# Splitting the second token half of a pair of d_ff tiles in one 768-wide piece, with sum and rectifier in one VectorE operation

## The chip, the core and the metric

The kernel runs on one core of a Trainium2 chip. The metric is device microseconds of one execution, lower is better. The times are medians of several executions; the profile is of one execution of its own. In the profile PE is TensorE's matmul, PEld its weight load, DVE is VectorE, ACT is ScalarE, POOL is GpSimd and SP is SyncE, whose queue issues the DMAs.

## What is computed

```python
def _moe_ref(x, w_in, w_out, s, b):      # 2304 tokens, d_model 512, d_ff 2048
    h = x @ w_in
    r = np.maximum(h, 0.0)
    g = s * (r * r) + b
    return g @ w_out
def _moe2_ref(x, w_in, w_out, alpha):
    h = x @ w_in
    g = np.maximum(h, 0.0) + alpha * np.minimum(h, 0.0)
    return g @ w_out
def reference(...):
    x = attention over a window of 64 (batch 4, 8 heads, 576 positions, head size 64)
    return _moe2_ref(_moe_ref(x, ...), ...)
```

So: a windowed attention, then layer one (code: layer 0; rectifier, then a square), then layer two (code: layer 1; a leaky rectifier with a slope for each d_ff unit). Activations stand transposed, with d_ff or d_model on the 128 partitions and tokens along the free axis.

## The kernel before

**Split operands.** Each fp32 operand of a matmul is split in a rounded high part and a low part (value minus high part), and a product is three matmuls: high by high, high by low, low by high. For a tile of the hidden activation g the split is a copy that rounds (`gh`, line 1048) and a subtraction (`gl`, line 1051), both in `halves`.

**Stages.** From 0 to about 240 us the attention and two d_ff groups of layer one run block by block (lines 1336 and 1396 hold their matmuls). From there on the work goes in *pairs*: two d_ff tiles of 128 by two token halves of 384 tokens are one pair, and `hidden_pair` computes its four 128 x 384 results of `x @ w_in` with seven half-size products instead of eight (`product`, matmuls on line 978, six matmuls each). Three token passes q of 768 tokens run over each d_ff group. Layer one has five such pairs in each pass (groups of 4, 2 and 4 tiles), 15 in all; layer two has four in groups 0 and 1, 12 in all, and another 12 in groups 2 and 3, which take a path of their own (`seven`) with seven products in the second matmul too.

**Inside a pair.** The products accumulate in four PSUM banks: two of a ring of two buffers (`b1`, `b4`, in the profile the tile `h`), and the two halves of a tile of its own (`hb`, in the profile `ab`). ACT copies between them (line 989): `b1` to `hb` half 0, `b4` to SBUF (`p5`), `hb` half 0 to half 1, `hb` half 1 to `b4`. At the end the first token half of the pair lies in `b1` (first d_ff tile) and `b4` (second tile), and the second token half is `hb` plus `p5`: a 768-wide DVE addition (line 1006) writes it to `both`, a stretch of 768 columns of the SBUF area `aq`, 384 for each d_ff tile. A PSUM buffer of the ring is given to the next pair once its last reader has run.

**After it, layer one.** `square` calls `squared` for each of the four 384-wide results: rectifier (line 1058, ACT or DVE) into a tile `r`, square in place (line 1062, ACT or DVE), then `halves`. In layer two `lrelu` calls `leaky` (a scaled copy on ACT, line 1075, and a DVE operation, line 1078, into `r`) and then `halves`. `g_place` gives the 768 columns for high and low part in the area `ax`.

**Second matmul.** `project` (line 1419) multiplies a tile's `gh` and `gl` with w_out, 12 matmuls for each tile of 128 x 384, about 1.7 pairs behind the pair that made it, and `sums` adds the PSUM result to the output (lines 1492 to 1499).

**Weights.** w_in and w_out arrive as float64; `converted` loads one tile (line 664, 512 KB, three buffers), ACT reads both words (lines 668 and 672, both wait for the load), DVE makes the exponent (lines 677 and 678), joins the words (682) and adds them (687). A buffer is free for the load after next but one when line 687 has run. w_out of layer one is then scaled (738 on ACT, 741 on DVE) and added up on POOL (733).

**Order.** Nothing waits for a free engine at run time. `Plan.step` takes the ways in which a step can run (engine and assumed cost), what it reads and writes, and a due time `at`; `emit` goes through all steps once and fixes both the engine and the order on each engine. A change of one step's cost or number thus moves others. On the chip every engine runs its list strictly in order.

Of the kernel before, what the change touches and what calls it, by code (L numbers as in the profile page):

```python
# [8 lines left out]

F32 = mybir.dt.float32  # L10
F32R = mybir.dt.float32r
# [3 lines left out]
AF = mybir.ActivationFunctionType  # L15
# [3 lines left out]
P = 128  # L19
# [5 lines left out]
HALF = 384  # L25
# [6 lines left out]
HURRY = 12.0  # L32
# [6 lines left out]
GRING = 10  # L39
# [19 lines left out]
def f32(ap):  # L59
    return ap.bitcast(F32)  # L60
# [188 lines left out]
def tile_window_attention_two_mlps(  # L249
# [14 lines left out]
    nc = tc.nc  # L264
# [27 lines left out]
    T = Plan()  # L292
# [4 lines left out]
    XA = area("ax", 8 * NT)  # L297
# [7 lines left out]
    XW = 4 * HALF  # L305
# [15 lines left out]
    def act(cols, fn):  # L321
        return ("act", 0.2 + cols * 0.00084, fn, 0.0)

    def dve(cols, fn, fast=False, port=False):
        return ("dve", 0.15 + cols * (0.00053 if fast else 0.00106), fn, 0.0) + (True,) * (fast or port)
# [15 lines left out]
    for g in range(SPLIT[0]):  # L341
        for bi in range(NB):
            n = blocks[bi][1]
# [13 lines left out]
    with tc.manual_schedule():  # L357
# [49 lines left out]
        for x, kind in enumerate(ROW):  # L407
            if x != 2 and kind == "mm":
                T.step([("pool", 0.35, lambda x=x: nc.gpsimd.tensor_copy(caps[:, x, :], caps[:, 2, :]), 0.0)],
                       reads=["caps2"], writes=[f"caps{x}"], at=-15.0, after=CONST_AT)  # L410
# [407 lines left out]
        C = 2 * HALF  # L818
        x2 = lambda ap: ap.rearrange("p (k c) -> p k c", k=2)
# [127 lines left out]
        def hidden_pair(layer, g, q, p):  # L947
            fs = groups[layer][g]
            n = number[layer, g, p]
            pr = f"{layer}.{g}.{q}.{p}"  # L950
            t0 = begin[layer, g, q] + p * unit(layer, g)
            slot = unit(layer, g) / 7
            seven = (layer, g) in SEVEN
# [12 lines left out]
            p5 = T.place("p5." + pr, AQ, 4 * HALF + n % 2 * HALF, HALF)  # L966
# [20 lines left out]
            def copy(out, src, reads, writes, order):  # L987
# [14 lines left out]
            copy(b4_, b3_, [hb3], [b4], 4)  # L1002
            product(4, 6, b4_, b4, False)
            both = T.place("c." + pr, AQ, C, C)
            T.step(
                [dve(C, lambda: nc.vector.tensor_add(  # L1006
                    x2(T[both]), T["hb"][:, :, :HALF],
                    T[p5].rearrange("p (o c) -> p o c", o=1).to_broadcast([P, 2, HALF])))],
                reads=[hb2, hb3, p5], writes=[(both, 0), (both, 1)], at=t0 + 5 * slot - HURRY,
            )  # L1010
            c_ = lambda x: (lambda: T[both][:, x * HALF:(x + 1) * HALF])
            f1, f2 = fs[2 * p], fs[2 * p + 1]
# [8 lines left out]
            for c, i, f, hk, hn, order in outs:  # L1021
                at = t0 + order * slot
                if seven:
                    leaky(f"B{(c if f == f1 else 3 - c)}.{g}.{q}.{p}", f, hk, hn, at)
                elif layer == 1:
                    g_place(layer, g, q, c, i, f)
                    lrelu(g, q, c, i, f, hk, hn, at)
                else:
                    g_place(layer, g, q, c, i, f)
                    square(q, c, f, hk, hn, at)  # L1030

        ORDER = (1, 5, 6, 2, 7, 3, 4)

        def g_place(layer, g, q, c, i, f):
            key = f"{layer}.{2 * q + c}.{f}"
            if i == 0 and c == 0:
                g_place.n += 2 * len(groups[layer][g])
            n = g_place.n + c * len(groups[layer][g]) + i
            G = T.place("g" + key, XA, 7 * XW + n % GRING * 2 * HALF, 2 * HALF, F32R)
            gh, gl = "gh" + key, "gl" + key  # L1040
            T.parts[gh] = T.parts[gl] = G
            T.tiles[gh], T.tiles[gl] = (lambda: T[G][:, :HALF]), (lambda: T[G][:, HALF:])

        g_place.n = 0

        def halves(key, r, rn, n, at):
            gh, gl = "gh" + key, "gl" + key
# [20 lines left out]
        def square(q, c, f, hk, hn, at):  # L1068
            squared(f"0.{2 * q + c}.{f}", hk, hn, HALF, at)

        def leaky(r, f, hk, hn, at):
            leaky.n += 1
            r2 = T.place(f"r2.{leaky.n}", AQ, leaky.n % 2 * HALF, HALF)
            rn, r2n = (lambda: T[r][:, :HALF]), (lambda: T[r2])
            T.step([act(HALF, lambda: nc.scalar.activation(r2n(), hn(), AF.Identity, scale=slope[:, f:f + 1]))],
                   reads=[hk, "side"], writes=[r2], at=at - HURRY)
            T.step(
                [dve(HALF, lambda: nc.vector.scalar_tensor_tensor(
                    out=rn(), in0=hn(), scalar=side[:, f:f + 1], in1=r2n(), op0=ALU.mult, op1=ALU.max), port=True)],
                reads=[hk, r2, "side"], writes=[r], at=at - HURRY,  # L1080
            )
# [93 lines left out]
        def pieces(layer, g, q, p):  # L1175
            ring = (layer, g) != SEVEN[-1] or q != turns[layer, g][-1]
            arena, off = ((AR, 0), (AR, 8 * HALF))[p]
            for x, n, src, reads, order in (
# [5 lines left out]
                s = 7 * p + x  # L1184
                key = f"G{x}.{g}.{q}.{p}"
                if ring:
# [10 lines left out]
        def output(layer, g, q, a):  # L1197
# [11 lines left out]
            def product(j, order, to, start, cols=(slice(0, HALF),), keys=None):  # L1209
# [3 lines left out]
                def mms(c):  # L1213
                    for p in range(2):
                        W = T[f"V{w}.{g}.{p}"].rearrange("p (h c) -> p h c", h=2)
                        G = T[f"G{first}.{g}.{q}.{p}"].rearrange("p (s h c) -> p s h c", h=2, c=HALF)[:, x - first]
                        for y, (s, h) in enumerate(((0, 0), (0, 1), (1, 0))):
# [328 lines left out]
        for g in range(SPLIT[0]):  # L1546
            for i, f in enumerate(groups[0][g]):
                for part in range(2):
                    at = FIRST_W[2 * i + part] if g == 0 else begin[0, g, 0] + (i + 2 * part) * pace[g, 0] - 12.0
# [23 lines left out]
        for x, (layer, g) in enumerate(order_of):  # L1573
# [3 lines left out]
            for p in range(len(fs) // 2):  # L1577
                n = number[layer, g, p]
                at = t + p * PAIR
# [5 lines left out]
            for i, f in enumerate(fs if (layer, g) not in SEVEN else ()):  # L1585
                at = t + LAG * PAIR + i * PAIR / 4 - 12.0 - 15.0 * end
# [88 lines left out]
```

## Time and profile before

| | |
|---|---|
| median of 3 runs | 842.8 us (842.38 to 844.94) |
| profiled execution | 840.98 us |
| its span, first to last instruction | 839.2 us |
| PE busy / PEld busy | 824.7 us (98%) / 775.7 us (92%) |
| DVE busy | 693.1 us (83%) |
| ACT busy | 536.9 us (64%) |
| POOL busy | 106.1 us (13%) |
| chain that ended last | PE 76%, DVE 10%, DMA 6%, ACT 3%, POOL 3% |
| granted TensorE clock | 1.000 of full speed throughout |

Read it by stages: the table by engine averages over the attention, whose start has waits, and the pairs. The windows of the trace give each engine's busy time in a stretch, the list of waits says for whom an engine stood idle, and the timeline gives one instruction after the other.

### The profile page before, as it was taken

The page shows a single profiled execution, that of the slowest core. Times are in us where ns is not written, and L with a number is a line of the kernel's source. Part 1 is how long each engine was busy: PE and PEld are TensorE (multiplying, and loading weights), DVE is VectorE, ACT ScalarE, POOL GpSimd, SP SyncE. Part 2 cuts the span into 40 slices and gives each one's busy share as a digit, 9 for nine tenths or more (in the row PEclk, how much of TensorE's full clock was granted, in tenths as well). Part 3 has the DMA queues.
Part 4 walks back from the last instruction along what each step waited for, and adds up shares of the span by engine and source line. Part 5 has one row for each costly group of instructions (what it writes and reads, how often), then busy time and mean ns, then how long its engine had stood idle before and what let it go on. Part 6 is the DMA issues. An engine that isn't in the chain of part 4 may idle for free.

```text
span 839.2 us, 15002 instructions
## 1 busy us (share of the span) xinstructions
PE 824.7 (98%) x5517; PEld 775.7 (92%) x5521; DVE 693.1 (83%) x1210; ACT 536.9 (64%) x1219; POOL 106.1 (13%) x117
## 2 busy tenths in 40 slices
PE   8899999999999999999999999999999999999997
PEld 4678878888899999999999999999999999999997
DVE  6978799698987887699888999878888688778695
ACT  6878997554676555477648678778655345445461
POOL 6443344442011010011000000000000000000000
PEclk9999999999999999999999999999999999999999
DMA  8576974467558989958799668858998667438813
GB/s 287 183 229 176 297 222 131 184 235 284 212 204 314 376 312 316 411 186 339 282 382 380 227 248 309 320 183 303 345 389 314 230 225 268 123 121 338 319 42 109
DMA packets 72648, 217.25 MB, mean 259 GB/s; under 512 B 7424, under 2 KB 25984, under 8 KB 72576
## 3 DMA queue, kind: packets, MB, share of 16 engines
q1 hardware_dynamic: 72576, 216.31, 71.8%
q8 instruction: 43, 0.70, 0.3%
q14 instruction: 29, 0.24, 0.1%
HBM read 151.00 MB, written 65.27 MB: 258 GB/s over the span
## 4 chain that ended last, share of the span: by engine, by line
PE 76%; DVE 10%; DMA 6%; ACT 3%; POOL 3%; issue 1%; SPq 0%; DVEq 0%; POOLq 0%; ACTq 0%
PE y L1419 23%; PE h L978 17%; PE ab L978 13%; PE y L1218 11%; DMA raw<-w_in 3%; PE h L1336 3%; DMA xd<-aq 3%; PE y L1396 3%; PE y L628 2%; PE y L597 2%; PE ab L523 1%; DVE aq L699 1%; ACT as__86 L562 1%; POOL as__86 L580 1%; DVE ag L1051 1%
## 5 line engine op out<-in xcount | busy, mean ns | idle before, releaser
L1419 PE MATMUL y<-ax,woh 128*128 128x384 f32 x864 | 196.2, 334 | 0.0
L978 PE MATMUL h<-ax,aw 128*128 128x384 f32 x936 | 184.4, 334 | 0.7 <-ACT h L989 0.6
L978 PEld LDWEIGHTS h<-ax,aw 128*128 128x128 f32 x936 | 164.2, 188 | 1.6 <-ACT h L989 0.9
L1419 PEld LDWEIGHTS y<-ax,woh 128*128 128x128 f32 x864 | 153.7, 188 | 0.5 <-DVE ay L1496 0.3
L978 PE MATMUL ab<-ax,aw 128*128 128x384 f32 x702 | 139.7, 335 | 1.1 <-ACT h L989 0.9
L978 PEld LDWEIGHTS ab<-ax,aw 128*128 128x128 f32 x702 | 123.1, 188 | 2.4 <-ACT h L989 1.6
L1419 PE MATMUL y<-ax,wol 128*128 128x384 f32 x432 | 121.2, 334 | 0.0
L1336 PE MATMUL h<-ax,aw 128*128 128x512 f32 (+1 forms) x360 | 83.9, 377 | 1.1 <-DVE ax L646 1.1
L1419 PEld LDWEIGHTS y<-ax,wol 128*128 128x128 f32 x432 | 79.0, 188 | 0.0
L1336 PEld LDWEIGHTS h<-ax,aw 128*128 128x128 f32 x360 | 62.0, 189 | 12.8 <-DVE ax L646 1.5
L1051 DVE TENSOR_TENSOR ax<-r,ax 128x384 fp32r<-128x384 f32 x108 | 57.9, 553 | 5.7 <-ACT ax L1048 5.2
L668 ACT ACTIVATE raw<-raw 128x512 f32<-128x512 f32 x64 | 43.2, 679 | 28.8 <-DMA raw<-w_in 16.5
L1006 DVE TENSOR_TENSOR aq<-ab,aq 128x768 f32<-128x768 f32 x39 | 37.3, 955 | 15.7 <-PE ab L978 11.9
L1062 ACT ACTIVATE r<-r 128x384 f32<-128x384 f32 (+2 forms) x90 | 47.5, 543 | 1.1
L580 POOL TENSOR_TENSOR as__86<-as__86,den 128x512 f32<-128x512 f32 x36 | 40.3, 1142 | 56.2 <-DVE den L573 34.1
L682 DVE SCALAR_TENSOR_TENSOR raw<-raw 128x512 int32<-128x512 int32 x64 | 46.3, 725 | 1.2 <-ACT raw L672 1.2
L1058 ACT ACTIVATE r<-h 128x384 f32<-128x384 f32 (+2 forms) x57 | 29.7, 521 | 27.4 <-PE h L1336 17.6
L1499 DVE TENSOR_TENSOR ay<-y,ay 128x384 f32<-128x384 f32 x72 | 37.7, 553 | 9.6 <-PE y L1419 9.5
L733 POOL TENSOR_TENSOR wsum<-wsum,raw 128x512 f32<-128x512 f32 x15 | 21.9, 1459 | 181.6 <-DVE raw L687 180.1
L687 DVE CUSTOM_DVE_ANT_0 raw<-raw 128x1024 uint16<-128x1024 uint16 x64 | 44.7, 704 | 0.1
L672 ACT ACTIVATE raw<-raw 128x512 int32<-128x512 uint32 x64 | 43.0, 680 | 2.4 <-DMA raw<-w_in 1.6
L1218 PE MATMUL y<-ax,woh 128*128 128x384 f32 (+1 forms) x183 | 41.3, 333 | 0.6 <-ACT y L1232 0.6
(164 smaller groups left out, 1493.7 us busy)
## 6 DMA issues: line engine op xcount, KB each, us to landing
ax<-xd SPq DMA_DIRECT2D x91, 768.0 KB, 6.3
aw<-wd SPq DMA_DIRECT2D x33, 512.0 KB, 5.1
raw<-w_in SPq DMA_DIRECT2D x32, 512.0 KB, 6.9
raw<-w_out SPq DMA_DIRECT2D x32, 512.0 KB, 5.5
xd<-ax SPq DMA_DIRECT2D x21, 768.0 KB, 4.5
wd<-ag SPq DMA_DIRECT2D x30, 512.0 KB, 6.6
xd<-aq SPq DMA_DIRECT2D x12, 768.0 KB, 4.1
xd<-ax SPq DMA_DIRECT2D x36, 192.0 KB, 4.6
```

Of the source, the lines that this page charges most:

```text
L580: eng.tensor_mul(x, x, d)
L668: [act(512, lambda: nc.scalar.activation(T[t], H().bitcast(F32), AF.Abs, scale=65536.0))],
L672: [act(512, lambda: nc.scalar.activation(L(), L().bitcast(U32), AF.Copy, scale=2.0 ** -29))],
L682: [dve(512, lambda: nc.vector.scalar_tensor_tensor(out=L(), in0=H(), scalar=-0x80000000, in1=L(), op0=ALU.bitwise_and, op1=ALU.bitwise_or) ...
L687: [dve(512, lambda: nc.vector.tensor_tensor(ti(), ti(), L(), op=ALU.add), port=True)],
L978: nc.tensor.matmul(bank(), W[:, wj, a, kt * P:(kt + 1) * P], X[:, c, kt, :], start=start and kt == 0 and y == 0, stop=kt == 1 and y == 2, ...
L1051: [dve(n, lambda: nc.vector.tensor_sub(T[gl], rn(), f32(T[gh])), port=True)],
L1062: [act(n, lambda: nc.scalar.activation(rn(), rn(), AF.Square)), dve(n, lambda: nc.vector.tensor_mul(rn(), rn(), rn()), port=True)],
L1218: nc.tensor.matmul(v(to)[:, c], W[:, s, a * P:(a + 1) * P], G[:, h, c], start=start and p == 0 and y == 0, stop=p == 1 and y == 2, skip_gr ...
L1336: nc.tensor.matmul(T[ps][:, :n].rearrange("p (c t) -> p c t", t=P), T[w][:, k * P:(k + 1) * P], T[X(x, k)], start=st, stop=sp,)
L1419: nc.tensor.matmul(ps, T[w][:, m * P:(m + 1) * P], T[x], start=(i == 0 and j == 0), stop=(last and j == 2), skip_group_check=closing(layer ...
L1499: ways = [dve(n, lambda a=a, yn=yn: nc.vector.tensor_add(a(), yn(), a()))]
```

## The change

In the pairs of layer one and of groups 0 and 1 of layer two, the second token half (`c == 1`, the two halves of `both`) is no longer split tile by tile. `joined` does it once for both d_ff tiles, 768 columns wide: in layer one a square in place in `both`, then one copy to both high parts and one subtraction to both low parts. In layer one the 768-wide addition into `both` becomes the operation TENSOR_ADD_SAT, max(min(a + b, infinity), 0), so that the two rectifiers go. In layer two `leaky` still runs on each tile, but writes its result in place into `both`. The first token half and groups 2 and 3 of layer two are written as before. Lines up to 1004 of the kernel before stand one line lower after; 1048, 1051, 1058, 1062, 1419 and 1462 become 1081, 1084, 1091, 1095, 1452 and 1495, and the addition becomes line 1010 (DVE instruction ISA), the 768-wide square 1049, copy 1057 and subtraction 1060.

```diff
+            def total():
+                x, y = T["hb"][:, :, :HALF], T[p5].rearrange("p (o c) -> p o c", o=1).to_broadcast([P, 2, HALF])
+                if layer == 0:
+                    nc.vector._custom_dve(TENSOR_ADD_SAT, out=x2(T[both]), in0=x, in1=y, s0=float("inf"), s1=0.0)
+                else:
+                    nc.vector.tensor_add(x2(T[both]), x, y)
+
             T.step(
-                [dve(C, lambda: nc.vector.tensor_add(
-                    x2(T[both]), T["hb"][:, :, :HALF],
-                    T[p5].rearrange("p (o c) -> p o c", o=1).to_broadcast([P, 2, HALF])))],
+                [dve(C, total)],
                 reads=[hb2, hb3, p5], writes=[(both, 0), (both, 1)], at=t0 + 5 * slot - HURRY,
             )
...
+                elif c == 1:
+                    g_place(layer, g, q, c, i, f)
+                    if layer == 1:
+                        leaky(hk, f, hk, hn, at, hn)
                 elif layer == 1:
...
+            if not seven:
+                joined(layer, q, f1, f2, both, t0 + 5 * slot)
+
+        def joined(layer, q, f1, f2, both, at):
+            reads, r = [(both, 0), (both, 1)], lambda: T[both]
+            if layer == 0:
+                T.step(
+                    [act(C, lambda: nc.scalar.activation(r(), r(), AF.Square)),
+                     dve(C, lambda: nc.vector.tensor_mul(r(), r(), r()), port=True)],
+                    writes=reads, at=at - HURRY,
+                )
+            keys = [f"{layer}.{2 * q + 1}.{f}" for f in (f1, f2)]
+            off = g_place.off[keys[0]]
+            assert g_place.off[keys[1]] == off + C
+            half = lambda h: XA[:, off:off + 2 * C].bitcast(F32R).rearrange("p (x h c) -> p h x c", h=2, c=HALF)[:, h]
+            ways = [act(C, lambda: nc.scalar.copy(half(0), x2(r()))), dve(C, lambda: nc.vector.tensor_copy(half(0), x2(r())), fast=True)]
+            T.step(ways[:1] if layer == 1 else ways, reads=reads, writes=["gh" + k for k in keys], at=at - HURRY)
+            T.step(
+                [dve(C, lambda: nc.vector.tensor_sub(half(1), x2(r()), f32(half(0))), port=True)],
+                reads=reads + ["gh" + k for k in keys], writes=["gl" + k for k in keys], at=at - HURRY,
+            )
...
-        def leaky(r, f, hk, hn, at):
+        def leaky(r, f, hk, hn, at, to=None):
             leaky.n += 1
             r2 = T.place(f"r2.{leaky.n}", AQ, leaky.n % 2 * HALF, HALF)
-            rn, r2n = (lambda: T[r][:, :HALF]), (lambda: T[r2])
+            rn, r2n = to or (lambda: T[r][:, :HALF]), (lambda: T[r2])
```

Of the 15 squares of 768 columns all go to ACT; of the 15 wide copies of layer one 13 go to DVE and 2 to ACT, and the 12 of layer two to ACT. PE's list of steps is the same up to the first pair and from the last pairs of group 1 of layer two on (803 of 985 steps in), and holds the same matmuls in between, partly in another order. At three places the lists of ACT and DVE read as follows.

**Place 1a, ACT, end of the first pair.** Before, in order: the scaled w_out, the two reads of a loaded w_in tile (tile `raw`), rectifier and square of the result in `b1` (tile `h`), the copy of `hb` half 1 to `b4`, and then the two reads of the w_in tile loaded next:

```order
L738 ACTIVATE woh_2790<-raw,s_sb 128x512
L668 ACTIVATE raw<-raw 128x512
L672 ACTIVATE raw<-raw 128x512
L1058 ACTIVATE r<-h 128x384
L1062 ACTIVATE r<-r 128x384
L989 COPY h<-ab 128x384
L668 ACTIVATE raw<-raw 128x512
L672 ACTIVATE raw<-raw 128x512
L1058 ACTIVATE r<-aq 128x384
```

The same place after (line 673 is before's 672, 669 its 668, 1091 its 1058, 1095 its 1062, 990 its 989):

```order
L739 ACTIVATE woh_2786<-raw,s_sb 128x512
L669 ACTIVATE raw<-raw 128x512
L673 ACTIVATE raw<-raw 128x512 x2
L1091 ACTIVATE r<-h 128x384
L669 ACTIVATE raw<-raw 128x512
L1095 ACTIVATE r<-r 128x384
L990 COPY h<-ab 128x384
L1091 ACTIVATE r<-h 128x384
L1049 ACTIVATE aq<-aq 128x768
```

Both reads of the tile loaded next have moved: one ahead of the rectifier of `b1`, one between the rectifier and its square.

**Place 1b, DVE, the same end of the first pair.** Before: the word additions of a w_out tile (687) and, after four output sums (1462) and a scaled low part (741), exponent, `gh` copy, the addition into `both` (1006) and `gl` subtraction:

```order
L677 TENSOR_SCALAR raw<-raw 128x512
L678 TENSOR_SCALAR raw<-raw 128x512
L741 SCALAR_TENSOR_TENSOR wol_2777<-raw,s_sb,woh_2763 128x512
L687 ISA raw<-raw 128x1024
L1462 TENSOR_TENSOR ay<-y_2695,ay 128x512
```

```order
L741 SCALAR_TENSOR_TENSOR wol_2814<-raw,s_sb,woh_2790 128x512
L677 TENSOR_SCALAR raw<-raw 128x512
L678 TENSOR_SCALAR raw<-raw 128x512
L1048 CAST ax<-r 128x384
L1006 TENSOR_TENSOR aq<-ab,aq 128x768
L1051 TENSOR_TENSOR ax<-r,ax 128x384
```

The same two pieces after (688 is 687, 1495 is 1462, 742 is 741, 678 and 679 are 677 and 678, 683 is 682):

```order
L742 SCALAR_TENSOR_TENSOR wol_2765<-raw,s_sb,woh_2755 128x512
L688 ISA raw<-raw 128x1024
L678 TENSOR_SCALAR raw<-raw 128x512
L679 TENSOR_SCALAR raw<-raw 128x512
L1495 TENSOR_TENSOR ay<-y_2696,ay 128x512
```

```order
L742 SCALAR_TENSOR_TENSOR wol_2812<-raw,s_sb,woh_2786 128x512
L678 TENSOR_SCALAR raw<-raw 128x512
L679 TENSOR_SCALAR raw<-raw 128x512
L683 SCALAR_TENSOR_TENSOR raw<-raw 128x512
L678 TENSOR_SCALAR raw<-raw 128x512
L679 TENSOR_SCALAR raw<-raw 128x512
L1081 CAST ax<-r 128x384
L1010 ISA aq<-ab,aq 128x768
L1084 TENSOR_TENSOR ax<-r,ax 128x384
```

One exponent pair (678, 679) has moved from ahead of the word addition 688 to behind it, and between the low part 742 and the `gh` copy 1081 stand a join (683) and another exponent pair more.

**Place 2, ACT, pairs of the two-tile group.** Before: rectifier, square and `gh` copy of `b1`, the two reads of a loaded w_in tile, the copy of `hb` half 1 to `b4`, the reads of the next tiles:

```order
L1058 ACTIVATE r<-h 128x384
L1062 ACTIVATE r<-r 128x384
L1048 CAST ax<-r 128x384
L668 ACTIVATE raw<-raw 128x512
L672 ACTIVATE raw<-raw 128x512
L989 COPY h<-ab 128x384
L668 ACTIVATE raw<-raw 128x512
L672 ACTIVATE raw<-raw 128x512 x2
```

After:

```order
L1091 ACTIVATE r<-h 128x384
L1095 ACTIVATE r<-r 128x384
L1081 CAST ax<-r 128x384
L669 ACTIVATE raw<-raw 128x512
L673 ACTIVATE raw<-raw 128x512
L669 ACTIVATE raw<-raw 128x512
L990 COPY h<-ab 128x384
L673 ACTIVATE raw<-raw 128x512 x2
```

The copy to `b4` now stands behind one read more, that of the next load.

## Rows read from the trace of the kernel before

**Rows 1.** Windows: stretch, its length, busy us (instructions) of each engine, clock, DMA.

```profile
240.00:680.00 440.00, 438.77 (x2526) 436.64 (x2525) 368.07 (x698) 290.62 (x578) 11.61 (x11) 1.00 0.82 309
680.00:820.00 140.00, 139.39 (x800) 138.18 (x799) 112.34 (x179) 71.14 (x133) 0.00 (x0) 1.00 0.55 193
```

**Rows 2.** Waits of PE, 240 to 680 us: us in total, times, longest.

```profile
PE ab L978 <- ACT h L989: 0.9, 1, 0.9
```

**Rows 3.** Groups by line and shape: count, busy us, mean ns, idle before and releaser.

```profile
L1058 ACT ACTIVATE r<-aq 128x384 f32<-128x384 f32 x30 | 14.3, 518 | 19.7 <-DVE aq L1006 19.5
...
L694 ACT CAST ax<-as__86 128x768 fp32r<-128x768 f32 x19 | 15.9, 839 | 1.4 <-DVE as__86 L913 1.0 <-DVE as__86 L1168 0.2 <-PE h L978 0.2
...
L1051 DVE TENSOR_TENSOR ax<-r,ax 128x384 fp32r<-128x384 f32 x108 | 57.9, 553 | 5.7 <-ACT ax L1048 5.2
L687 DVE CUSTOM_DVE_ANT_0 raw<-raw 128x1024 uint16<-128x1024 uint16 x64 | 44.7, 704 | 0.1
L1006 DVE TENSOR_TENSOR aq<-ab,aq 128x768 f32<-128x768 f32 x39 | 37.3, 955 | 15.7 <-PE ab L978 11.9 <-ACT h L989 3.7
```

**Rows 4.** Timeline of ACT, first pair: start us, us, instruction, idle before and releaser.

```profile
236.95 0.49 ACT L1058 ACTIVATE r<-h 128x384 f32<-128x384 f32 x1 [0.27 <-PE h L978]
237.47 0.53 ACT L1062 ACTIVATE r<-r 128x384 f32<-128x384 f32 x1
239.03 0.46 ACT L989 COPY h<-ab 128x384 f32<-128x384 f32 x1 [1.03 <-PE ab L978]
239.61 0.68 ACT L668 ACTIVATE raw<-raw 128x512 f32<-128x512 f32 x1
```

**Rows 5.** Timeline of DVE, first pair.

```profile
224.83 0.42 DVE L696 CAST aw<-as__86 128x512 fp32r<-128x512 f32 x1
...
231.54 1.52 DVE L677 TENSOR_SCALAR raw<-raw 128x512 f32<-128x512 f32 x1
233.09 0.43 DVE L678 TENSOR_SCALAR raw<-raw 128x512 int32<-128x512 int32 x1
...
234.09 0.69 DVE L687 CUSTOM_DVE_ANT_0 raw<-raw 128x1024 uint16<-128x1024 uint16 x1
234.69 2.48 DVE L1462 TENSOR_TENSOR ay<-y,ay 128x512 f32<-128x512 f32 x4
...
239.52 0.96 DVE L1006 TENSOR_TENSOR aq<-ab,aq 128x768 f32<-128x768 f32 x1 [0.62 <-ACT h L989]
240.40 0.55 DVE L1051 TENSOR_TENSOR ax<-r,ax 128x384 fp32r<-128x384 f32 x1
240.86 0.69 DVE L682 SCALAR_TENSOR_TENSOR raw<-raw 128x512 int32<-128x512 int32 x1
```

**Rows 6.** Timeline of PE, first pair.

```profile
238.83 2.24 PE L978 MATMUL h<-ax,aw 128*128 128x384 f32 x12
240.91 0.53 PE L1419 MATMUL y<-ax,woh 128*128 128x384 f32 x2
```

**Rows 7.** Tile raw, 225 to 245 us: ns min/median/max of a line; us from DMA issue to landing.

```profile
L677 DVE TENSOR_SCALAR raw<-raw x5: 414/420/1516, 228.7 to 241.5; 128x512 f32<-128x512 f32 x5
...
DMA to landing us min/median/max: 3.4/3.4/4.7
```

**Rows 8.** Timeline of POOL, first pair.

```profile
231.16 1.61 POOL L733 TENSOR_TENSOR wsum<-wsum,raw 128x512 f32<-128x512 f32 x1 [3.56 <-DVE raw L687]
234.92 1.30 POOL L733 TENSOR_TENSOR wsum<-wsum,raw 128x512 f32<-128x512 f32 x1 [2.15 <-DVE raw L687]
```

**Rows 9.** Timeline of ACT, a pair of the two-tile group.

```profile
356.51 0.67 ACT L668 ACTIVATE raw<-raw 128x512 f32<-128x512 f32 x1 [2.77 <-DMA raw<-w_in]
357.08 0.66 ACT L672 ACTIVATE raw<-raw 128x512 int32<-128x512 uint32 x1
357.63 0.48 ACT L989 COPY h<-ab 128x384 f32<-128x384 f32 x1
```

**Rows 10.** The page's DMA issues: KB each, median us from issue to landing.

```profile
raw<-w_in SPq DMA_DIRECT2D x32, 512.0 KB, 6.9
```

More of the change, by code (lines that the diff above doesn't have):

```diff
@@ L8 @@
 from concourse._compat import with_exitstack
+from concourse.dve_ops import TENSOR_ADD_SAT
 F32 = mybir.dt.float32
@@ L1038, in g_place @@
             n = g_place.n + c * len(groups[layer][g]) + i
-            G = T.place("g" + key, XA, 7 * XW + n % GRING * 2 * HALF, 2 * HALF, F32R)
+            g_place.off[key] = 7 * XW + n % GRING * 2 * HALF
+            G = T.place("g" + key, XA, g_place.off[key], 2 * HALF, F32R)
             gh, gl = "gh" + key, "gl" + key
@@ L1042, in g_place @@
             T.tiles[gh], T.tiles[gl] = (lambda: T[G][:, :HALF]), (lambda: T[G][:, HALF:])
-        g_place.n = 0
+        g_place.n, g_place.off = 0, {}
         def halves(key, r, rn, n, at):
```

## The prediction, made before the changed kernel was run

> **What bounds the kernel now.** I read the windows by stage first [rows 1]. All that the diff edits runs in the pairs, from about 240 us on. In the stretch from 240 to 680 us (pairs of layer one, then groups 0 and 1 of layer two) PE is busy for 438.77 of 440 us; the reader should see that DVE has 368.07 and ACT 290.62 there, so that both have spare time and PE none. In the last pairs (680 to 820 us) PE has 139.39 of 140. So all that PE could still gain in the pairs is 1.23 + 0.61 = 1.84 us, 0.22% of the run. Then the list of PE's waits [rows 2]: the largest by far in the first stretch is one wait of 0.86 us (shown as 0.9) for the ACT copy of `hb` half 1 to `b4`; the other 0.37 us of idle are crumbs. No matmul is added or taken away, and PE's own list is the same up to the first pair and from the last pairs of group 1 on. The work taken from ACT and DVE is therefore worth nothing by itself; what counts is whether some result now comes later to a PE that has no slack.
>
> **What goes away, off the path.** In layer one 30 rectifiers of 518 ns go from ACT (the first of [rows 3]), 15.5 us. Their 30 squares, on ACT the same kind of pass, become 15 of 768 columns; the nearest row for those is ACT's 768-wide cast, 839 ns, so 30 x 518 = 15.5 us become 15 x 839 = 12.6 us. 30 subtractions of 553 ns become 15 like the 768-wide addition at 955 ns: 16.6 to 14.3 us. The copies and the 12 pairs of layer two give a few us more of the same kind. Together some 20 us of ACT and 5 of DVE, all of it beside a full PE: 0 us on the path. The cover is PE's 438.77 of 440; without it, that is where PE idles for this work, the gain could at most be the 1.84 us.
>
> The trace bears out on ACT that one wide pass costs less than two narrow ones (839 against 2 x 518 ns). The Trainium skill (VectorE: DVE Perf Modes, section "The TRN2 errata — SBUF-src ops pay a fixed extra latency per instruction") gives a reason for DVE and recommends few large operations; by that rule alone one would forecast a faster kernel. The price of an instruction agrees with it; the forecast does not, since no engine but PE is short of time [rows 1].
>
> **The new operation, TENSOR_ADD_SAT.** No run before has it. Nearest rows: the stock addition of the same shape, 955 ns, and the custom word addition, 704 ns for 512 result words (1.37 ns each; 768 of them would take 1,056 ns) [rows 3]. I take 955, the row of the same shape. Bounds: 0.96 us less if it ran in no time, and 0.96 more if it took twice the stock time, each only where something waits for it at once, which is the first pair below; elsewhere the wide square and copy follow it and PE projects the result more than a pair later.
>
> **Place 1, the first pair (237 to 243 us): a new wait.** This is the largest term. Before, ACT runs rectifier and square of `b1` at 236.95 and 237.47, idles 1.03 us, copies to `b4` at 239.03, and only then reads the w_in tile loaded next, at 239.61 [rows 4]. After, the first read of that tile stands ahead of the rectifier, the second ahead of the square. ACT runs its list in order, so behind a late load stand the rectifier, the square, the copy to `b4` and all that reads them. When does the tile land? Its load is issued when its buffer is free, after the word addition at 234.09 to 234.78 [rows 5], and takes 3.4 us (median in this stretch) to 4.7 us (longest) to land [rows 7]; before, the longest is this one and it lands at about 239.5, with ACT's read right behind [rows 4]. After, the word addition comes earlier: an exponent pair, 0.42 + 0.43 us, has moved behind it. So issue at about 233.9 and landing at 237.4 (3.4 us) to 238.6 (4.7 us). The rectifier starts about 0.6 us after that, at 238 to 239.2 instead of 236.95. The next pair's first products (PE, 238.83 [rows 6]) need the PSUM buffer that the rectifier reads, and the copy to `b4`, two instructions of 0.5 to 0.6 us further on, ends at about 239.6 to 240.8, where it ended at 239.5.
>
> DVE has a delay of its own. Ahead of the `gh` copy, the addition into `both` and the `gl` subtraction now stand one join (about 0.6 us from start to start; 0.69 long) and one more exponent pair (0.8 us), and the pair moved behind the word addition runs beside POOL's L733, which began at 234.92 for 1.30 us [rows 8], once the word addition is done. In the trace an exponent half that ran beside such a POOL operation (231.54, POOL 231.16 to 232.77) took 1,516 ns where the others take 414 to 420 [rows 5, 7, 8]: a pair of 1.9 instead of 0.8 us. So the `gl` subtraction, at 240.40 before [rows 5], starts at 240.40 - 0.9 (earlier word addition) + 1.9 (pair beside POOL) + 0.6 + 0.8 - 0.6 (idle before the addition, now filled) = 242.2, 1.8 us later. PE's projection of this tile starts at 240.91 without idle [rows 6], just behind the subtraction's end; I charge 1.7 us. The ACT delay (1 to 1.7 us) runs beside it, and the two do not add. Bounds: 0.5 us, if POOL's operation misses the pair and the load lands in 3.4 us; 2.7 us, with a TENSOR_ADD_SAT of twice the time as well.
>
> The Trainium skill (SBUF — State Buffer, section "SBUF: two separate sides") says that DVE and GpSimd share a port pair under an exclusive lock and that the loser blocks fully. The 1,516 ns agree. By it the pair waits for whatever POOL has left and place 1 costs the 1.7 us; without it, 0.6 us.
>
> **Place 2, a pair of the two-tile group (357 us).** This is the 0.86 us of [rows 2]: ACT waited 2.77 us for a w_in load, read the tile at 356.51 and 357.08, and only then made the copy to `b4` at 357.63 [rows 9]. After, one read more stands ahead of that copy, worth 0.57 us (356.51 to 357.08). If all else stays, PE waits 0.86 + 0.57; if PE comes later by place 1 while the load does not, the 0.86 goes. Loads are issued by SP in order, behind transfers that hang on earlier results, so I take the first: +0.6, bounds -0.9 and +0.8 (two reads late, or a load a little later).
>
> **The crumbs.** The other 0.37 us: half of them close while PE waits elsewhere, -0.2. The 680 to 820 stretch I leave at 0.
>
> **Sum.** 1.7 + 0.6 - 0.2 = 2.1 us. The profiled execution took 840.98 us with a span of 839.2; after, 843.1 with a span of 841.3. The median of the runs shown is 842.8, 1.8 above the profiled one; the difference goes on it: **844.9 us**. Bounds of the terms: 0.5 - 0.9 - 0.4 = -0.8 and 2.7 + 0.8 = 3.5, so 842.0 to 846.3.
>
> **Rivals.**
>
> A, slower still: the load decides place 1. In the whole run a w_in load takes a median of 6.9 us [rows 10], not 3.4. Issued at 233.9 it would land at 240.8; rectifier at 241.4, copy to `b4` ending at about 243, 3.5 us later than before, and PE has only the older pair's projections in between. With place 2 at +0.8: about +4.3, up to 4.9 if the subtraction then meets the next reads, 847 to 847.7 us. It decides from a landing later than about 239. For it: that very load was slow (4.7 us). Against: others in the stretch took 3.4 [rows 7].
>
> B, faster: both places cost nothing, because PE has older projections ready and the shorter ACT list empties sooner, and the idle 1.84 us come back: 841.0. Against: it is the whole idle time [rows 1], and place 1 has no slack at 240.91 [rows 6].
>
> C, the operation does not do what it says at the stated price: it takes 1.9 us. +0.96 at place 1, hidden elsewhere: 845.8 us.
>
> D, nothing moves: the delays lie under PE's queue of older projections, 842.8.
>
> **How the numbers follow.** About 0.3%, 2.5 us, is what a measurement of this kernel can tell from no change. The forecast (0.40), D (0.16) and small forms of B lie mostly within it. A (0.28), C (0.08) and the upper third of the forecast go beyond: slower 0.38. Faster than 2.5 us is more than all idle of the pairs, so it needs something that I do not see: 0.06. Same: 0.56. The range takes in B (841.0) and A to 848.0.
>
> **What would show it.** Place 1: PE waits between 238 and 245 us that before had none, for the rectifier (line 1091, ACT) or the `gl` subtraction (1084, DVE); ACT idle ahead of 669 for the load. Place 2: PE's wait for the copy (990, ACT) near 357 us at 1.4 us instead of 0.86. The costs: line 1010 at 955 ns, 1049 at 839 ns, 1060 at 955 ns; ACT busy down by some 18 us. Wrong if PE's idle from 240 to 680 us stays at or below 1.2 us (B or D), if place 1 costs over 3 us (A), or if the change shows elsewhere, say as a PE wait for `gh` or `gl` of `both` in later pairs or a lower granted clock than the 1.00 of [rows 1].

## The result, and the profile after

| | before | after |
|---|---|---|
| median | 842.8 us (841.79 to 844.94, 11 runs) | 847.17 us (845.72 to 853.02, 11 runs) |
| ratio to before, 95% interval | | 1.0056 (1.0036 to 1.0077) |
| profiled execution / its span | 840.98 / 839.2 us | 847.17 / 845.1 us |
| ACT busy / DVE busy | 536.9 / 693.1 us | 516.2 / 691.6 us |

The change costs 0.56%, 4.7 us (3.0 to 6.5). The two traces differ by more, 5.9 us of span: the trace of before is of an execution 1.8 us under its median, that of after is one at its median. The trace tells where, the medians how much. The granted TensorE clock does not explain the loss: the six executions of the kernel after with a mean of 1.000 have a median of 846.1 us, and the 29 such executions of the kernel before that the experiments below recorded one of 841.6.

Windows of the kernel after, by stage, with the columns of [rows 1]:

```profile
240.00:680.00 440.00, 434.76 (x2496) 431.54 (x2495) 361.77 (x658) 266.97 (x509) 11.63 (x11) 1.00 0.82 304
680.00:820.00 140.00, 138.93 (x798) 137.83 (x797) 112.27 (x178) 70.33 (x134) 0.00 (x0) 1.00 0.57 204
```

ACT is busy 23.7 us less from 240 to 680 us (290.62 before; 20.7 us less in the whole run), and PE idles 5.24 us there where it idled 1.23. From 680 to 820 it is 1.07 against 0.61. Together 4.5 us. The rest is mostly in how a busy PE is modelled: in [rows 6] 12 matmuls without a wait show 2.24 us busy, though the next one starts 2.08 us after the first, so each wait hides some 0.16 us more than its idle time; and six matmuls behind a wait show 1.31 us where six others show 1.20. For six waits more that is 1.0 and 0.7 us. The sum, 6.2, meets the 5.9 us to 0.3.

Waits of PE after, 240 to 680 us (in total, times, longest), where [rows 2] had one:

```profile
PE h L979 <- DVE r L1111: 2.0, 2, 1.1
PE h L979 <- ACT h L990: 1.7, 2, 1.3
PE y L1452 <- DVE ax L1084: 0.7, 1, 0.7
PE h L979 <- ACT r L1091: 0.4, 1, 0.4
PE ab L979 <- ACT h L990: 0.3, 1, 0.3
```

The same in order of time (start, us, then in brackets the idle time before):

```profile
240.86 1.31 PE L979 MATMUL h<-ax,aw 128*128 128x384 f32 x6 [0.40 <-ACT h L990]
243.09 0.44 PE L1452 MATMUL y<-ax,woh 128*128 128x384 f32 x1 [0.74 <-DVE ax L1084]
...
302.12 1.31 PE L979 MATMUL h<-ax,aw 128*128 128x384 f32 x6 [0.37 <-ACT r L1091]
...
360.50 1.34 PE L979 MATMUL ab<-ax,aw 128*128 128x384 f32 x6 [0.35 <-ACT h L990]
409.81 1.33 PE L979 MATMUL h<-ax,aw 128*128 128x384 f32 x6 [1.28 <-ACT h L990]
...
557.98 1.34 PE L979 MATMUL h<-ax,aw 128*128 128x384 f32 x6 [0.85 <-DVE r L1111]
...
622.58 1.31 PE L979 MATMUL h<-ax,aw 128*128 128x384 f32 x6 [1.13 <-DVE r L1111]
```

The first two are place 1, 360 is place 2. The other four, 3.63 us in all, are none of the places that the prediction priced. None of them waits for a result of `joined` as such; what PE lacks is `b1` or `b4`, which the change doesn't touch. ACT shows why. Ahead of the wait at 409.81, which is for the copy in the last row:

```profile
406.49 0.67 ACT L669 ACTIVATE raw<-raw 128x512 f32<-128x512 f32 x1 [1.82 <-DMA raw<-w_in]
...
407.74 0.66 ACT L669 ACTIVATE raw<-raw 128x512 f32<-128x512 f32 x1 [0.17 <-DMA raw<-w_in]
408.31 0.49 ACT L1081 CAST ax<-r 128x384 fp32r<-128x384 f32 x1
408.71 0.67 ACT L673 ACTIVATE raw<-raw 128x512 int32<-128x512 uint32 x1
409.28 0.47 ACT L990 COPY h<-ab 128x384 f32<-128x384 f32 x1
```

and ahead of those at 557.98 and 622.58, where line 1108 is the scaled copy on which DVE's line 1111 waits:

```profile
553.11 0.66 ACT L669 ACTIVATE raw<-raw 128x512 f32<-128x512 f32 x1 [3.72 <-DMA raw<-w_out]
...
556.58 0.58 ACT L1108 ACTIVATE aq<-h,slope 128x384 f32<-128x384 f32 x1
```

```profile
620.75 0.66 ACT L669 ACTIVATE raw<-raw 128x512 f32<-128x512 f32 x1 [3.24 <-DMA raw<-w_in]
621.31 0.56 ACT L1108 ACTIVATE aq<-h,slope 128x384 f32<-128x384 f32 x1
```

Each time ACT stands 1.8 to 3.7 us for a weight load (3.4 us ahead of the wait at 302 too), with a step queued behind it that PE needs. At 302, 558 and 623 us the reads stand earlier in ACT's list than before: three of them ahead of the step that PE needs where there was one, four where there were two, one where there was none. That an ACT with less to do gave the list-maker (`Plan.step` and `emit`) room for this is likely, but not shown. At 410 us no read has moved ahead. Before, the same three reads stood ahead of this copy; the load, issued at nearly the same time (393.5 and 393.9 us), landed 3.6 us earlier (402.8 and 406.4), and 18 matmuls of line 1419 stood between the two products into `h`, where after there are none. The first read and the second product of before there, ACT and PE:

```profile
402.84 0.67 ACT L668 ACTIVATE raw<-raw 128x512 f32<-128x512 f32 x1 [0.45 <-DMA raw<-w_in]
410.54 1.20 PE L978 MATMUL h<-ax,aw 128*128 128x384 f32 x6
```

Over 240 to 680 us, ACT's waits at the first read of a loaded tile, of after and then of before:

```profile
ACT raw L669 <- DMA raw<-w_out: 17.9, 5, 5.3
ACT raw L669 <- DMA raw<-w_in: 13.2, 9, 3.2
```

```profile
ACT raw L668 <- DMA raw<-w_in: 11.3, 7, 4.0
ACT raw L668 <- DMA raw<-w_out: 9.5, 6, 2.8
```

31.1 us in place of 20.8. The operations themselves, by line and shape (count, busy us and mean ns, then the idle time before):

```profile
L1060 DVE TENSOR_TENSOR ax<-aq,ax 128x768 fp32r<-128x768 f32 x27 | 25.7, 951 | 0.0
...
L1010 DVE CUSTOM_DVE_ANT_1 aq<-ab,aq 128x768 f32<-128x768 f32 x15 | 14.3, 953 | 8.4 <-PE ab L979 7.0 <-ACT raw L673 1.4
L1049 ACT ACTIVATE aq<-aq 128x768 f32<-128x768 f32 x15 | 12.6, 842 | 9.1 <-DVE aq L1010 9.1
```

TENSOR_ADD_SAT takes 953 ns, as long as the stock addition (955 [rows 3]): the rectifier costs nothing more.

### The profile page after: what moved, and what is told of

The parts are those of the page before. It is cut to its first block, busy times and chain, and to the rows that moved or that the text cites. A ratio compares the mean times of both kernels' runs of the same rounds, so it can differ in the third digit from the quotient of the medians.

```text
span 845.1 us, 14896 instructions
## 1 busy us (share of the span) xinstructions
PE 826.9 (98%) x5521; PEld 775.6 (92%) x5521; DVE 691.6 (82%) x1175; ACT 516.2 (61%) x1155; POOL 106.6 (13%) x117
## 4 chain that ended last, share of the span: by engine, by line
PE 68%; DVE 12%; DMA 12%; ACT 3%; POOL 3%; issue 2%; SPq 0%; DVEq 0%; POOLq 0%; ACTq 0%
PE y L1452 20%; PE h L979 15%; PE ab L979 12%; PE y L1251 10%; DMA raw<-w_out 4%; DMA xd<-aq 4%; PE h L1369 3%; DMA raw<-w_in 3%; PE y L1429 3%; PE y L629 2%; PE y L598 2%; PE ab L524 1%; DVE aq L700 1%; DVE raw L683 1%; POOL as__86 L581 1%
## 5 line engine op out<-in xcount | busy, mean ns | idle before, releaser
L1275 DVE TENSOR_TENSOR ay<-y,ay 128x384 f32<-128x384 f32 (+1 forms) x49 | 26.7, 547 | 17.8 <-PE y L1251 11.9
L1265 ACT COPY y<-y 128x384 f32<-128x384 f32 x36 | 16.7, 465 | 39.5 <-PE y L1251 23.8
L1108 ACT ACTIVATE aq<-h,slope 128x384 f32<-128x384 f32 x48 | 27.8, 580 | 20.5 <-PE h L979 15.9
```

## Experiments

Two theories: **order** (the loss comes from what the change moves in the lists of ACT and DVE) and **operations** (it comes from the wide operations, which hand over both d_ff tiles together, or from TENSOR_ADD_SAT). Ratios are to the kernel before on the same chip.

**Order and operations taken apart.** Two kernels cross the two. The first keeps after's order on every engine and puts before's operations at its places (`rectify_square` is a rectifier and a square for each half, `twice` the operation for each half; the subtraction is doubled likewise):

```diff
-                if layer == 0:
-                    nc.vector._custom_dve(TENSOR_ADD_SAT, ...)
-                else:
-                    nc.vector.tensor_add(x2(T[both]), x, y)
+                nc.vector.tensor_add(x2(T[both]), x, y)
...
-                    [act(C, lambda: nc.scalar.activation(r(), r(), AF.Square)),
+                    [act(C, rectify_square),
...
-            ways = [act(C, lambda: nc.scalar.copy(half(0), x2(r()))), ...
+            ways = [act(C, lambda: twice(nc.scalar.copy, 0)), ...
```

> The changed kernel with its order kept step for step on every engine, but with the narrow operations of before at the same places: a stock 768-wide addition, then at the place of the wide square two 384-wide rectifiers and two squares on ACT, at the place of the wide copy two copies, at that of the wide subtraction two subtractions. Theory 'order' (the time was lost because ACT's reads of weight tiles now stand ahead of steps that PE waits for): the loss stays, 847 us (846 to 849, since the narrow work behind a late load is some 1 us longer at the few places where PE waits). Rival 'operations' (the wide operations, or TENSOR_ADD_SAT, deliver results later): back to about 843 (842 to 844.5).

Measured: 850.49 us, ratio 1.0103 (1.0086 to 1.0120). The loss stayed and grew, beyond what either theory said (849 at most). In its trace PE's waits for `b1` and `b4` in the pairs are there, two groups of them with 2.3 + 2.1 = 4.4 us where the kernel after has 0.3 + 0.4 (its fifth and fourth row above), since two rectifiers and two squares stand in ACT's list where one square stood:

```profile
PE ab L979 <- ACT h L990: 2.3, 2, 1.6
PE h L979 <- ACT r L1099: 2.1, 3, 1.5
```

In this order, then, the wide operations are worth 0.47%, some 4 us (the two intervals do not meet): behind a late load, work on ACT counts. The second kernel keeps before's order and has after's operations, each wide one at the place of the second of the two narrow ones:

```diff
-            T.step([act(n, lambda: nc.scalar.activation(rn(), hn(), AF.Relu)), ...
+            T.step([act(n, lambda: j or nc.scalar.activation(rn(), hn(), AF.Relu)), ...
...
-                [act(n, lambda: nc.scalar.activation(rn(), rn(), AF.Square)),
+                [act(n, lambda: j[1]("sq", lambda: nc.scalar.activation(b_(), b_(), AF.Square)) if j
+                     else nc.scalar.activation(rn(), rn(), AF.Square)),
```

> The kernel before with its order kept step for step on every engine, but with the changed kernel's operations: TENSOR_ADD_SAT as addition, both rectifiers left out, one wide square, copy and subtraction at the place of the second of the two narrow ones. Theory 'order': as before, 842.8 us (841.5 to 844), PE's waits those of before (0.86 us near 358 us). Rival 'operations': 846 to 847, with PE waits that before did not have.

Measured: 842.7 us, ratio 1.0003 (0.9987 to 1.0019). The operations cost nothing, and gain nothing either, as a full PE lets one expect. PE's waits were not those of before, though: the profiled execution has 3.0 us of PE idle from 240 to 680 us, with a longest wait of 1.6 us at place 2. So **operations** falls; **order** stands.

**What in the order.** Loads made small, with all instructions of PE, ACT, DVE and POOL in their places:

```diff
+        FIRST = lambda at: 128 if at > 220.0 else 1024
...
-                dma(1, P * 4096, lambda: nc.sync.dma_start(out=T[raw], in_=src)),
+                dma(1, P * 4096, lambda: nc.sync.dma_start(out=T[raw][:, :FIRST(at)], in_=src[:, :FIRST(at)])),
```

> The changed kernel, same instructions in the same order on PE, ACT, DVE and POOL; only the weight loads of the pairs (due after 220 us) fetch an eighth of the tile, 64 KB of 512, so that they land early. Left out: seven eighths of these weights. Theory 'late loads' (ACT stands for a load with steps queued behind it that PE needs): PE's waits at 240.9 (0.40 us shown), 302 (0.37), 410 (1.28), 558 (0.85) and 623 us (1.13) go; with what each costs beyond the idle shown, some 0.16 us, that is 4.8 us: about 842.5 (841 to 844). Rival 'list length' (ACT simply has too much queued ahead of these steps, whatever the loads do): the waits stay within half, 845 to 847. The 0.74 us wait for the low part at 243 us, at the end of DVE's chain, stays by both or falls by at most half.

> The control: the kernel before with the same small loads. Theory 'late loads': only its wait of 0.86 us near 358 us goes (about 1 us): 841.8 (840.5 to 843). If fewer bytes by themselves made the kernel faster, through other transfers, it would gain as much as the changed kernel does, 4 us or more.

Measured: after 839.98 us, ratio 0.9973 (0.9960 to 0.9986); before 838.79 us, ratio 0.9969 (0.9948 to 0.9990). The loads were earlier, not all early: ACT still stands 11.3 us at first reads, in place of 31.1. So far the two ratios are level; the medians are 1.2 us apart, about what place 1, which stays, costs (below). The changed kernel gains 0.83%, the kernel before 0.31%: more than the 1 us that I expected, so fewer bytes seem to help a little by themselves. The 0.52% between the two gains, 4.4 us, is then what the late loads cost the change; by the intervals of the three ratios it can be 1.7 to 7 us. Of after's waits those at 302, 360, 410, 558 and 623 us are gone, and from 240 us on these are left:

```profile
240.78 1.32 PE L981 MATMUL h<-ax,aw 128*128 128x384 f32 x6 [0.91 <-ACT h L992]
...
243.03 0.45 PE L1454 MATMUL y<-ax,woh 128*128 128x384 f32 x1 [0.74 <-DVE ax L1086]
```

They are place 1, where I had expected the first of them to go: a late load is not what holds that place. (Line 992 is after's 990, 1086 its 1084.)

**Place 1.** The rows of the kernel after there, ACT, DVE, POOL:

```profile
238.05 0.67 ACT L673 ACTIVATE raw<-raw 128x512 int32<-128x512 uint32 x1 [1.78 <-DMA raw<-w_in]
238.62 0.47 ACT L1091 ACTIVATE r<-h 128x384 f32<-128x384 f32 x1
239.34 0.68 ACT L669 ACTIVATE raw<-raw 128x512 f32<-128x512 f32 x1 [0.24 <-DVE wol L742]
239.93 0.51 ACT L1095 ACTIVATE r<-r 128x384 f32<-128x384 f32 x1
240.34 0.47 ACT L990 COPY h<-ab 128x384 f32<-128x384 f32 x1
```

```profile
231.14 1.40 DVE L679 TENSOR_SCALAR raw<-raw 128x512 int32<-128x512 int32 x1
...
234.78 1.41 DVE L679 TENSOR_SCALAR raw<-raw 128x512 int32<-128x512 int32 x1
236.11 2.47 DVE L1495 TENSOR_TENSOR ay<-y,ay 128x512 f32<-128x512 f32 x4
238.50 0.74 DVE L742 SCALAR_TENSOR_TENSOR wol<-raw,s_sb,woh 128x512 fp32r<-128x512 f32 x1
...
242.49 0.55 DVE L1084 TENSOR_TENSOR ax<-r,ax 128x384 fp32r<-128x384 f32 x1
```

```profile
230.91 1.34 POOL L734 TENSOR_TENSOR wsum<-wsum,raw 128x512 f32<-128x512 f32 x1 [3.70 <-DVE raw L688]
```

Counted in matmuls, the place cost 1.65 us. After the 12 products into `ab` come 30 matmuls of 384 columns, though not in the same order. Before, they take from 238.83 [rows 6] to 244.42, 5.59 us; after, from 238.91 (2.08 us behind 236.83) to 246.15, 7.24 us. PE, the first row of before, the others of after:

```profile
244.42 1.20 PE L978 MATMUL ab<-ax,aw 128*128 128x384 f32 x6
236.83 2.24 PE L979 MATMUL ab<-ax,aw 128*128 128x384 f32 x12
246.15 1.20 PE L979 MATMUL h<-ax,aw 128*128 128x384 f32 x6
```

Two holds in a row. The load lands at 238.0 and lets the rectifier go at 238.62. But the read at 239.34, which stands ahead of the square and the copy to `b4`, waits for DVE's low part of a w_out tile (line 742): the read writes the buffer that 742 reads. And DVE is late because the exponent half, 0.43 us elsewhere, takes 1.40 and 1.41 us while POOL adds (POOL's second addition began at 234.55). Two kernels leave POOL's additions out, one of them with the small loads as well; the edit takes out those of w_out tiles 6 to 15, not only the four that the expectations name:

```diff
-                else:
+                elif f < 6:
                     nc.gpsimd.tensor_add(wsum, wsum, T[t])
```

> The changed kernel, same order, without POOL's four additions of w_out tiles 6 to 9 to the running sum (left out: these terms of the bias). It asks what holds the first pair up (240 to 243 us), where the small loads changed nothing: the waits of PE there were 0.91 us for the copy to b4 and 0.74 us for the low part. Theory 'POOL': the exponent halves that took 1.40 and 1.41 us beside POOL's additions take 0.43, DVE is some 1 us earlier from 236 us on, ACT's read of the next tile, which waits for DVE's line 742, too, and PE's wait for the low part (0.74) goes; its wait for the copy to b4 stays at 0.2 to 0.4, since the load of the other tile still lands at 237.9. Gain some 0.8 us. Rival 'list': the chain of DVE is as long without POOL, because its sums wait for PE anyway; both waits stay.

> The same with the small loads beside it (left out: those terms of the bias, and seven eighths of the weights due after 220 us). Theory 'POOL': now both waits of PE at the first pair go, or fall below 0.2 us each, and PE idle from 240 to 680 us falls from 1.55 us to about 0.3. Rival 'list': 1.2 us or more stay at the first pair.

Without POOL's additions, large loads:

```profile
232.16 0.43 DVE L679 TENSOR_SCALAR raw<-raw 128x512 int32<-128x512 int32 x1
...
236.40 0.74 DVE L742 SCALAR_TENSOR_TENSOR wol<-raw,s_sb,woh 128x512 fp32r<-128x512 f32 x1
```

```profile
238.74 2.24 PE L979 MATMUL h<-ax,aw 128*128 128x384 f32 x12
```

The half takes 0.43 us, line 742 runs 2.1 us earlier, and both waits of place 1 are gone, also the one that I had expected to stay; ACT's read no longer stood for the load until 238, but ran at 235.6, since the buffer was free earlier. Yet that run took 846.22 us, about as long as the kernel after. PE comes to the later places sooner, the loads by less: at 360 us PE by 2.3 us and the read by 1.8, so that this wait is 0.79 us instead of 0.35; and at 604 us, where ACT's read of a late load comes only 0.5 us sooner, a new wait of 0.95 us stands:

```profile
604.45 1.31 PE L979 MATMUL h<-ax,aw 128*128 128x384 f32 x6 [0.95 <-DVE r L1111]
```

With the small loads beside it the run took 837.61 us, and the gain of place 1 stays; PE idles 0.64 us from 240 to 680:

```profile
240.00:680.00 440.00, 439.36 (x2534) 438.29 (x2534) 363.31 (x663) 270.43 (x512) 0.00 (x0) 1.00 0.73 266
```

These two are single runs: their rows settle place 1; their times, only the direction.

**Another order.** The list-maker assumes that a weight load lands 2 us after its transfer time. One number makes it assume 5 us, so that the reads stand later, in both kernels:

```diff
-                dma(1, P * 4096, lambda: nc.sync.dma_start(out=T[raw], in_=src)),
+                dma(1, P * 4096, lambda: nc.sync.dma_start(out=T[raw], in_=src), 5.0),
```

> The changed kernel with one number changed: the order is made with the assumption that a weight load lands 3 us later than assumed so far, so that ACT's two reads of a loaded tile stand later in its list. Theory 'order': the waits of PE at 302, 410, 558 and 623 us, all behind an ACT that stood for a load, go; PE idle from 240 to 680 us falls from 5.2 us to 2 or less, 843 us (841 to 845). Rival 'operations': the waits stay, 846 to 848.

> The kernel before with the same number changed, as the control for the run of the changed kernel with it. Theory 'order': the one wait of 0.86 us near 358 us goes, 842 us (840.5 to 843.5), and the changed kernel with the same number is level with it within 1 us. Rival 'operations': 842 here too, but the changed kernel stays 3 us or more above.

Measured: after 847.36 us, 1.0066 (1.0050 to 1.0082); before 849.29 us, 1.0090 (1.0074 to 1.0106). As times both were missed, and the changed kernel is not level with the other but 1.9 us shorter (the intervals just overlap), the opposite of what **operations** said. In the trace of the first, the stretches 0 to 240 and 240 to 680 us tell why:

```profile
0.00:240.00 240.00, 227.23 (x2074) 180.95 (x2079) 198.70 (x307) 170.21 (x498) 92.85 (x104) 0.99 0.65 216
240.00:680.00 440.00, 439.27 (x2531) 438.02 (x2530) 370.01 (x668) 272.92 (x516) 12.40 (x12) 1.00 0.82 306
```

The pairs do what was expected, 0.73 us of PE idle in place of 5.24. But the number also moved the attention's steps, and PE is busy 4.5 us less there than before (231.71). The next two hold the edit to loads due after 220 us (`5.0 if at > 220.0 else 2.0`):

> The changed kernel with the order made for weight loads that land 3 us later, but only for loads due after 220 us, so that the attention keeps its order. Theory 'order': the run of the changed kernel in which all loads were assumed late had 0.73 us of PE idle from 240 to 680 us in place of 5.24, and lost the gain before 240 us. Here the loss before 240 us goes: 842.7 (841.5 to 844). Rival 'operations': 846 or more.

> The kernel before with the same. Theory 'order': it has 1.23 us of PE idle from 240 to 680 us to win or to shuffle: 842.5 (841 to 845), and the changed kernel with the same edit is within 1.5 us of it. Rival 'operations': the changed kernel stays 3 us or more above this one.

Measured: after 844.48 us, 1.0023 (1.0006 to 1.0041); before 845.41 us, 1.0028 (1.0015 to 1.0041). The two are level, as **order** said, though each is 0.4 to 0.5 us beyond the time expected of it. The changed kernel got back more than half of its loss; in its trace the four waits are gone, and two others, of 1.67 us at 224 and 1.45 us at 392 us, for output sums of DVE, have come in. The kernel before, with no operation changed, lost 0.28% by a new order alone. Its trace has 3.25 us of PE idle from 240 to 680 us in place of 1.23, and the granted clock adds to it: behind waits of PE of 0.61, 1.01 and 0.43 us between 387 and 392 us it fell to 0.50, the lower level (1.2 GHz), and two matmuls of line 1419 on 384 columns, 0.51 us elsewhere, took 0.84:

```profile
392.00:394.00 2.00, 2.00 (x7) 2.00 (x7) 2.00 (x6) 0.07 (x1) 0.00 (x0) 0.50 1.05 400
```

All 12 executions of it have a mean granted clock of 0.994 to 0.998. The 28 such executions of the kernel before that were recorded have a median of 843.5 us, the 29 at 1.000 one of 841.6: differences of 0.2% can be those of the clock. Then 4.0 and 3.0 in place of 5.0:

> The changed kernel with the order made for loads (due after 220 us) that land 2 us later than assumed, where 3 us gave a ratio of 1.0023. Theory 'order': the time is set by which steps happen to stand behind a wait, so 840.5 to 846, no waits of ACT's reads at the four old places; a version under the kernel before is possible (0.2% at most, the idle time of the pairs). Rival 'operations': not under 845.

> The same with 1 us later. Theory 'order': between the changed kernel (1.0056) and the ones above, 841 to 847, with waits at some of the old places where a load takes over 4.4 us. Rival 'operations': 847.

Measured: 840.83 us, 0.9979 (0.9963 to 0.9995), and 841.42 us, 0.9985 (0.9973 to 0.9998), both near the lower end of what was expected, and slightly under the kernel before. ACT's standing at first reads in the trace of the first falls to 5.0 us, from 31.1. PE of the first, 240 to 680 us, idles 1.19 us:

```profile
240.00:680.00 440.00, 438.81 (x2529) 437.36 (x2527) 367.55 (x666) 274.11 (x519) 12.29 (x12) 1.00 0.83 311
```

That version is shorter than both kernels, than the one before by 0.2%. It is the best of three settings, so part of it may be choice, and 0.2% is also what the clock can make; whether the kernel before would gain as much from 4.0 was not tried.

## Why the prediction was right in sign and half in size

It said 844.9 us, 2.1 more; measured were 847.17, 4.4 to 4.7 more, inside the range of 841.0 to 848.0. The likeliest case, within 0.3%, did not come; slower, which came with 0.56%, had 0.38.

- **The bound**: right. PE is full, the work taken away is worth nothing by itself (842.7 us with the operations alone), and every us lost is a wait of PE.
- **Costs of the operations**: right. 953 ns for TENSOR_ADD_SAT (taken as 955), 842 for the square (839), 951 for the subtraction (955), ACT 20.7 us less (20). DVE fell by 1.5 us in place of 5. Rival C is out.
- **Place 1, +1.7**: right, 1.65 us counted in matmuls, of which 0.40 + 0.74 = 1.14 show as idle. The low part started at 242.49, forecast 242.2; the rectifier at 238.62, forecast 238 to 239.2. The step of POOL's addition was right, and it decides the place. The step "When does the tile land?" had the landing right (238.0, forecast 237.4 to 238.6), but it is not what decides: the wait that I had overlooked is the read's own for a buffer that DVE frees. What the runs agree with here is the port lock that the prediction cited from the Trainium skill (SBUF — State Buffer, section "SBUF: two separate sides"): an exponent half takes 1.40 us beside POOL and 0.43 without it, and without it the waits of place 1 are gone.
- **Place 2, +0.6**: wrong in sign, -0.5 (0.35 us in place of 0.86). The read does stand ahead of the copy, and the load came later too, by 1.6 us (first read at 358.14 instead of 356.51); but PE came later still, by 2.9 us (ready at 360.15 instead of 357.30), through place 1 and the wait at 302. That is in part the case that the prediction named as its lower bound and did not take.
- **The crumbs, -0.2**: this step failed, and it is the largest. The other pairs were not searched for moved reads; I stopped at the places where the trace of before showed a wait or a missing cushion. The mechanism that place 1 was costed with, a read moved ahead of a step that PE needs, stood at three places more, 302, 558 and 623 us: 0.37, 0.85 and 1.13 us. Each could be found in the lists: a read of `raw` ahead of line 1091 or 1108. The fourth, 1.28 us at 410 us, is a load that landed later, ahead of a copy for which PE, whose own list had changed, comes sooner; that PE's list changes there was known and not followed up. The four together are 3.63 us.
- **The stretch from 680 us, 0**: 0.46 us more, a wait for a transfer of `vd` at 771.
- **Rival A** had the price (847 to 847.7 us) and the mechanism, but put it nearly all at place 1; what it adds to the forecast happened elsewhere, and in smaller pieces. That the range held is in part luck: its upper end was made from a late load at place 1.

Open: why the load at 410 us landed later, and why single executions of one order differ in these waits, as the one of before's order with wide operations did. In part it is the granted clock: in the trace of the order made with 3.0, of an execution of 845.11 us, it is 0.50 (1.2 GHz) from 24 to 26 us, and PE was busy for 0.88 us from 20 to 22 us; in the trace of the kernel before, with 1.28 us there, it stays at 1.00.

## What to carry to other kernels

When one engine is full and the others run fixed lists, the value of a shorter operation is what the new order makes of it. Look in each in-order list for instructions that wait for a transfer, note what has moved behind them, and ask of each whether the full engine needs it within the time by which that transfer may be late; do this along the whole list, not only where a wait shows already. To tell an operation from the order it brings, run each operation in the other's order: here two kernels settled it.

## What was not expected of the hardware

- The rectifier in TENSOR_ADD_SAT costs nothing measurable: 953 ns for 768 columns from PSUM and SBUF, the stock addition 955.
- Over the 64 weight loads of 512 KB of the kernel after, the time from issue to landing ranges from 3.4 to 12.5 us, with a median of 5.9:

```profile
DMA to landing us min/median/max: 3.4/5.9/12.5
```

- Time won on the full engine ahead of late transfers was not kept here: without POOL's additions place 1 gave its waits back, and the run was no shorter (846.22 us) until the loads were made small too (837.61; single runs both).
- A wait of PE can cost more than its idle time: in the kernel before with later reads, waits of 0.61, 1.01 and 0.43 us were followed by a granted clock of 0.50 from 392 to 394 us. It need not: in the changed kernel with the same edit, waits of 0.55 and 1.45 us at the same place were followed by 1.00.
